# Six row tiles, DMA transposes and column tiles in a linear-attention and FFT-gate kernel on one core

## The chip, the core and the metric

The kernel runs on one core of one Trainium2 chip. The metric is the device time of one execution in microseconds (us). A core has a matrix engine (PE, with its weight loads shown as PEld), a vector engine (DVE), an activation engine (ACT), a general engine (POOL) and a queue engine (SP). They run their own instruction lists and wait for each other through semaphores. Matmul results go to PSUM, which DVE and ACT read; everything else works on SBUF. Transfers are issued from queues (here POOL's for loads, SP's and ACT's for stores) and carried by 16 DMA engines.

## What is computed

There are B = 8 batches, 8 heads, S = 576 positions and 64 columns a head, so 512 model columns. In the first half, attention without softmax:

```python
r = np.maximum(x, 0.0)
phi = np.concatenate([r * c, r * s], axis=-1)      # c, s: cosine and sine of the position
kv = np.einsum('bhsf,bhsd->bhfd', k_p, v)
z = np.sum(k_p, axis=2)
num = np.einsum('bhsf,bhfd->bhsd', q_p, kv)
den = np.einsum('bhsf,bhf->bhs', q_p, z)[..., None] + 1e-06
attn = num / den
```

In the second half, x is that result with its heads side by side, [8, 576, 512]:

```python
proj = x @ w_proj                                  # 512 x 1536
x1, x2, x3 = (three slices of 512 columns)
x2_conv = np.fft.irfft(np.fft.rfft(x2) * np.fft.rfft(filter), n=S)   # along the 576 positions
out = (x1 * x2_conv * x3) @ w_out
```

## The kernel before

The work is done batch by batch, and the batches are pipelined by hand: the order in which the program emits its pieces is, but for marked exceptions (`behind(...)` puts an instruction right after a marked one on its engine), the order of each engine. SBUF buffers and PSUM units (four, of two banks each) come from pools; a piece that asks for a buffer waits until its last reader is done.

Stages of a batch, with the names that the profile uses:

- **Loads.** POOL's queue loads q, k and v of a batch (`qraw`, `kraw`, `vraw`, L121) and casts them to f16. Position s = 6p + j lies in partition p, column group j.
- **phi** (L99, L97, on DVE): `kp` gets both halves by 12 instructions. `qp` gets a plain relu (one instruction of 3072 elements) and a second half scaled by the tangent (6 instructions).
- **kv** (L491): 48 matmuls for 8 heads; `va` is v with a column of ones beside it (copied by ACT, L128). ACT evicts to `kvs`.
- **qt** (L504): q is transposed by 48 matmuls against a permutation matrix `perm`, evicted in two overlapping halves by DVE (L511) and ACT (L515) into the single buffer `qpt`. The layout has five tiles of 128 columns, in which positions from the front and mirrored positions from the back stand side by side.
- **num** (L530): 40 matmuls, 5 tiles for each head. DVE adds epsilon, takes the reciprocal and multiplies into `att` (L536 to L540).
- **fx** (L556, L570, ACT L560, L574): matmuls against the small matrix `fm` transpose `att` and at the same time form 12 combinations of rows for a first radix-6 step of the FFT and 12 rows in plain order (front and back half). So one fold delivers both the operand of x2 and that of the gate.
- **x2** (L593): in three blocks of 96 rows and two components each, 24 matmuls of 512 columns. ACT scales into `x2f` (L598).
- **dft** (L607): 6 matmuls of 96x96 tables `tre` and `tim`; ACT copies to `xf`; DVE multiplies with the filter's spectrum `h3` (L612 to L617) into `yf`.
- **gate** (L630): x1 and x3 for four column groups, 64 matmuls of 288 columns. ACT copies x1 to f16 (`x1s`, L636); DVE multiplies it with x3, which it reads from PSUM (`g`, L638).
- **inv** (L656, L657): 32 matmuls with the inverse tables; ACT evicts to `eq` (L660); **y** (L672 to L677, DVE): even and odd sums (16 instructions of 144 elements for the four groups), the two halves, the product with `g`.
- **out** (L695): 20 matmuls against w_out on five row tiles, of which the last overlaps the one before; ACT evicts (L700), SP's queue stores in pieces that follow the row layout (L715).

The tables, among them those of the FFT, are computed on chip ahead of the loop. Batches 0 and 1 and the q part of batch 2 are emitted ahead of the loop, between the set-up pieces. The loop over b from 1 then emits x2 of b between num of b+1; dft of b; for each of the four column groups gate of b and fx of b+1; inv of b; out of b-1 between qt of b+2; kv of b+2; y of b. For the last batch `inv` is emitted ahead of the fourth gate, and its output tiles are evicted and stored tile by tile.

Of the kernel before, what the change touches and what calls it, by code (L numbers as in the profile page):

```python
# [17 lines left out]
def kernel(  # L18
# [15 lines left out]

    nc = tc.nc
# [6 lines left out]
    NT = 5  # L42
# [25 lines left out]
    tcol = consts.tile([128, NJ], FP32, tag="tcol", name="tcol")  # L68
    epsc = consts.tile([128, NT], FP32, tag="epsc", name="epsc")
    perm = consts.tile([NP, NP], FP16, tag="perm", name="perm")  # L70
# [5 lines left out]
    fm = consts.tile([128, 24, 10], FP16, tag="fm", name="fm")  # L76
    tre = consts.tile([NP, 3, NP], FP16, tag="tre", name="tre")
    tim = consts.tile([NP, 3, NP], FP16, tag="tim", name="tim")

# [9 lines left out]
    qpt_buf = [consts.tile([128, NH, NT, 2, 64], FP16, tag=f"qpt{i}", name=f"qpt{i}") for i in range(1)]  # L89
# [24 lines left out]
    raw_t = {}  # L114

    def load_qk(b, nm, hs=slice(0, NH)):
        src = {"q": q, "k": k, "v": v}[nm]
        if hs.start == 0:
            rw = work.tile([NP, NH, NJ * D], FP16, tag="raw", bufs=4, name=f"{nm}raw{b}")
            raw_t[(b, nm)] = rw  # L120
        nc.gpsimd.dma_start(  # L121
            out=raw_t[(b, nm)][:, hs], in_=src[b, hs].rearrange("h (p j) d -> p h (j d)", j=NJ)
        )

    def emit_va(b, xs=range(4)):
        for x in xs:
            hs = slice(2 * x, 2 * x + 2)
            nc.scalar.copy(  # L128
                out=va_buf[b % 2][:, hs, :, 0:D],
                in_=raw_t[(b, "v")][:, hs].rearrange("p h (j d) -> p h j d", j=NJ),  # L130
            )
# [28 lines left out]
    def emit_iotas(part):  # L160
# [13 lines left out]
        iota("sr_i", [NP, QS], lambda t: [(t, [[2, 3], [12, NP // 2]], 1, 0)])  # L174

    def emit_cols():
# [6 lines left out]
        nc.vector.memset(warm, 0.0)  # L183
        sj = cc["s6_i"]
# [3 lines left out]
        nc.vector.tensor_tensor(out=tcol, in0=tcol, in1=scol, op=AL.mult)  # L188

        u16 = small("u16p")  # L190
        rnd(u16, p, 1.0 / 16.0, -15.0 / 32.0)
        dest = small("dest")
        tsc(dest, p, 6.0, AL.mult)
        nc.vector.scalar_tensor_tensor(
            out=dest, in0=u16, scalar=-95.0, in1=dest, op0=AL.mult, op1=AL.add
        )
        tsc(perm, cc["nrow_i"], dest[0:NP], AL.is_equal)

    def emit_pads():
        for va in va_buf:  # L200
            nc.vector.memset(va[:, :, :, D : D + 2], 1.0 / A1)
        for t in qpt_buf:
            nc.vector.memset(t[:, :, :, 0, 60:64], 0.0)
            nc.vector.memset(t[:, :, :, 1, 0:4], 0.0)

    def emit_fm():

        p = cc["p"]
        loc = small("loc")
        side = small("side")  # L210
        nc.vector.tensor_copy(out=loc[0:64], in_=p[0:64])
        tsc(loc[64:128], p[64:128], -1.0, AL.mult, 127.0, AL.add)
        nc.vector.memset(side[0:64], 1.0)
        nc.vector.memset(side[64:128], -1.0)
        lo = small("lo")
        rnd(lo, loc, 1.0 / 6.0, -5.0 / 12.0)
        li = small("li")
        nc.vector.scalar_tensor_tensor(
            out=li, in0=lo, scalar=-6.0, in1=loc, op0=AL.mult, op1=AL.add
        )  # L220


        orb = small("orb", NT)
        for t in range(NT):
            tsc(orb[:, t : t + 1], lo, 10.0 * t, AL.add)
        oj = small("oj", NT)
        rnd(oj, orb, 1.0 / 16.0, -15.0 / 32.0)
        pos = small("pos", NT)

        tsc(pos, orb, 6.0, AL.mult)  # L230
        nc.vector.scalar_tensor_tensor(
            out=pos, in0=oj, scalar=-95.0, in1=pos, op0=AL.mult, op1=AL.add
        )
        nc.vector.scalar_tensor_tensor(
            out=pos, in0=li.to_broadcast([128, NT]), scalar=96.0, in1=pos, op0=AL.mult, op1=AL.add
        )
# [6 lines left out]
        orow_i = cc["orow_i"][:, 0:10]  # L243
        match = small("match", 10)
# [5 lines left out]
        for sl, (kk, c0) in enumerate([(0, 0.25), (3, 0.25), (1, 0.25), (1, 0.0), (2, 0.25), (2, 0.0)]):  # L250
# [4 lines left out]
        nc.scalar.activation(out=coef[:, 0:6], in_=ph, func=AF.Sin, scale=TWO_PI)  # L255
        tsc(coef[:, 3:6:2], coef[:, 3:6:2], 1.0 / R3, AL.mult)

        tsc(coef[:, 0:6], coef[:, 0:6], 2.0, AL.mult)
        tsc(coef[:, 0:6], coef[:, 0:6], RC, AL.add, -RC, AL.add)
        tsc(coef[:, 0:6], coef[:, 0:6], 0.5, AL.mult)  # L260
        tsc(coef[:, 6:12], coef[:, 0:6], side, AL.mult)
# [12 lines left out]
            in0=coef.unsqueeze(2).to_broadcast([128, 24, 10]),  # L274
            in1=match.unsqueeze(1).to_broadcast([128, 24, 10]),
# [23 lines left out]
    def emit_rows():  # L299
# [5 lines left out]
        par = cc["par"] = small("par")  # L305
        rnd(par, p, 0.5, -0.25)
        nc.vector.scalar_tensor_tensor(
            out=par, in0=par, scalar=-2.0, in1=p, op0=AL.mult, op1=AL.add
        )
# [10 lines left out]
    def emit_fwd_tables():  # L320
# [4 lines left out]
        u = small("u16")  # L325
        rnd(u, p, 1.0 / 16.0, -15.0 / 32.0)
        j = small("jr")
        nc.vector.scalar_tensor_tensor(
            out=j, in0=half, scalar=-3.0, in1=u, op0=AL.mult, op1=AL.add
        )  # L330
        w = small("w2s")

        tsc(w, p, 12.0, AL.mult, 1.0, AL.add)
        nc.vector.scalar_tensor_tensor(out=w, in0=u, scalar=-192.0, in1=w, op0=AL.mult, op1=AL.add)
        nc.vector.scalar_tensor_tensor(out=w, in0=j, scalar=2.0, in1=w, op0=AL.mult, op1=AL.add)
# [24 lines left out]
        for tb in (tre, tim):  # L360
            tsc(tb[:, 1:3], tb[:, 1:3], amp[0:NP], AL.mult)
            nc.vector.tensor_tensor(out=tb[:, 0], in0=tb[:, 0], in1=mask, op=AL.mult)

# [59 lines left out]
    def emit_h():  # L423
        hc, hs_, hb, alt = cc["hc"], cc["hs"], cc["hb"], cc["alt"]
        fa = filt16.rearrange("p x (j n) -> p x j n", j=3)
        for x, op in ((0, AL.add), (1, AL.subtract)):
# [5 lines left out]
        for bl in range(3):  # L432
# [15 lines left out]
            tsc(h3[:, bl, 1], u[0:NP, 1], sc, AL.mult)  # L448
            nc.vector.tensor_copy(out=h3[:, bl, 2], in_=h3[:, bl, 1])
        u = unit("h_nyq")  # L450
        for j in range(3):
            nc.tensor.matmul(
                u[0:1, 0], alt[:, j % 2 : j % 2 + 1], feo[:, 0, j], start=(j == 0), stop=(j == 2)
            )
        nc.scalar.activation(out=h3[0:1, 0, 2], in_=u[0:1, 0], func=AF.Copy, scale=1.0 / S)
# [4 lines left out]
    def emit_phi(b, nm, h0=0, nh=NH):  # L460
        rw = raw_t[(b, nm)]
        dst = kp_t if nm == "k" else qp_t
        if h0 == 0:
            dst[b] = work.tile([NP, NJ, NH, 2, D], FP16, tag=f"{nm}p", bufs=2 if nm == "q" else 1, name=f"{nm}p{b}")
        t = dst[b]
        if nm == "q":

            tsc(
                t[:, :, h0 : h0 + nh, 0],
                rw[:, h0 : h0 + nh].rearrange("p h (j d) -> p j h d", j=NJ), 0.0, AL.max,  # L470
            )
        for j in range(NJ):
            for cs, col in ((0, ccol), (1, scol)) if nm == "k" else ((1, tcol),):
                mark["phi", b, nm] = tsc(
                    t[:, j, h0 : h0 + nh, cs], rw[:, h0 : h0 + nh, ds(j * D, D)],
                    col[0:NP, j : j + 1], AL.mult, 0.0, AL.max,
                )
# [21 lines left out]
    def emit_qt(b, hp):  # L499
        qp, qpt = qp_t[b], qpt_buf[0]  # L500
        u = psum.tile([128, 2, 1024], FP16, tag="u", bufs=4, name=f"qt{b}_{hp}")
        for hh in range(2):
            for j in range(NJ):
                nc.tensor.transpose(  # L504
                    u[:, hh, ds(j * NP, NP)],
                    qp[:, j, 2 * hp + hh].rearrange("p a b -> p (a b)"),
                    perm,
                )
        hsl = slice(2 * hp, 2 * hp + 2)
        ev = nc.scalar.copy if b == 0 and hp < 2 else nc.vector.tensor_copy  # L510
        mark["qpt", b, hp] = ev(  # L511
# [368 lines left out]
```

## Time and profile before

| what | value |
|---|---|
| time, median of 3 | 272.12 us (272.1 to 272.9) |
| span of the profiled execution | 271.2 us |
| mean granted PE clock | 0.978 |
| busy share PE / DVE / ACT | 90% / 84% / 73% |
| length of a steady batch period | 28.5 us |
| DMA, mean over the span | 98 GB/s |

A busy share is an average over the whole span. Matmuls are pipelined, so a group's mean duration (for instance 286 ns for the gate's) is the way through the array, while the spacing of their starts is what a queue of them costs. Sums over a stretch of the chain of waits, divided by their number of instructions, give that spacing. Idle time in a group's row is that of its engine just ahead of the group, with what ended most of it.

### The profile page before, as it was taken

What the parts mean: (1) busy time and instruction counts of PE and PEld (TensorE: products, weight loads), DVE (VectorE), ACT (ScalarE), POOL (GpSimd) and SP (SyncE); (2) the same over time, 40 slices, a digit from 0 to 9 for tenths busy, and PEclk for the clock granted to TensorE, in tenths of its full rate; (3) what the DMA queues carried; (4) which work ended last, traced back from release to release, by engine and by line L of the source; (5) the groups of instructions that cost most, each with busy time, mean ns of one, the idle gap of its engine ahead of it and who ended that gap; (6) DMA issues with size and microseconds to landing.
All of it is one profiled execution on the core that took longest, in us unless ns stands there. A gap on an engine that the chain in (4) does not pass through costs nothing.

```text
span 271.2 us, 6320 instructions
## 1 busy us (share of the span) xinstructions
PE 243.0 (90%) x2457; PEld 175.2 (65%) x2457; DVE 226.9 (84%) x805; ACT 196.8 (73%) x274; POOL 27.3 (10%) x47
## 2 busy tenths in 40 slices
PE   0287998878989999999999999999999999999991
PEld 0164767547858776786678676867687768756830
DVE  7689997998899898979897989978997479646951
ACT  2279679798497778877897789786977667857630
POOL 8551111020020101110111011000000000000000
PEclk9999999995799999999999999999999999999998
DMA  5999998919019296636860868114000600060235
GB/s 79 168 206 205 206 205 122 166 14 169 3 14 161 33 230 90 89 40 152 150 101 3 174 128 124 16 51 125 0 2 9 169 2 0 2 174 13 69 117 155
DMA packets 26991, 26.70 MB, mean 98 GB/s; under 512 B 1680, under 2 KB 22160, under 8 KB 26960
## 3 DMA queue, kind: packets, MB, share of 16 engines
q0 software_dynamic: 21200, 16.84, 42.7%
q1 hardware_dynamic: 5120, 8.39, 10.7%
q10 hardware_dynamic: 640, 1.05, 1.3%
q8 instruction: 19, 0.31, 0.5%
q14 instruction: 12, 0.10, 0.1%
HBM read 33.69 MB, written 9.44 MB: 159 GB/s over the span
## 4 chain that ended last, share of the span: by engine, by line
PE 50%; ACT 22%; DVE 21%; DMA 4%; issue 1%; POOL 0%; SPq 0%; POOLq 0%; ACTq 0%
PE x L630 20%; PE x L593 9%; ACT x2f L598 7%; ACT va L128 7%; PE kv L491 5%; PE out L695 4%; PE fx L556 4%; DVE eo L672 4%; ACT fx L560 3%; DMA vraw<-in_v_dram 2%; DVE kp L99 2%; PE qt L504 2%; PE dft L607 2%; PE inv L657 2%; DVE qpt L511 2%; PE inv L656 2%
## 5 line engine op out<-in xcount | busy, mean ns | idle before, releaser
L630 PE MATMUL x<-fx,wp 128*128 128x288 f16 x512 | 67.5, 286 | 1.1 <-ACT fx L560 1.0
L630 PEld LDWEIGHTS <-wp 128*128 128x128 f16 x512 | 50.0, 98 | 13.3 <-issue 0.3
L593 PE MATMUL x<-wp,fx 128*96 128x512 f16 x192 | 45.2, 382 | 0.5 <-ACT x2f L598 0.5
L560 ACT CAST fx<-fx 128x960 f16<-128x960 f32 x32 | 30.6, 961 | 13.7 <-PE fx L556 13.7
L695 PE MATMUL out<-wo,y 128*128 128x512 f16 x160 | 37.6, 379 | 0.7 <-DVE y L677 0.7
L598 ACT ACTIVATE x2f<-x 96x1024 f16<-96x1024 f32 x24 | 24.5, 1020 | 14.6 <-PE x L593 14.6
L593 PEld LDWEIGHTS <-fx 128*96 128x96 f16 x192 | 22.4, 124 | 15.1 <-issue 0.8
L672 DVE TENSOR_TENSOR eo<-eq 128x144 f16<-128x144 f16 x128 | 23.7, 228 | 10.1 <-ACT eq L660 9.9
L128 ACT COPY va<-vraw 96x768 f16<-96x768 f16 x32 | 25.3, 827 | 9.3 <-DMA vraw<-in_v_dram 9.3
L638 DVE TENSOR_TENSOR g<-x,x1s 128x288 f16<-128x288 f32 x64 | 27.0, 448 | 1.3 <-PE x L630 1.1
L491 PE MATMUL kv<-va,kp 96*128 96x65 f16 x384 | 16.4, 202 | 11.7 <-ACT va L128 8.8
L540 DVE TENSOR_TENSOR att<-num,rcp 128x640 f16<-128x640 f32 x32 | 26.1, 820 | 0.3
L515 ACT COPY qpt<-qt 128x600 f16<-128x600 f16 x32 | 20.4, 671 | 7.5 <-DVE qpt L511 7.5
L695 PEld LDWEIGHTS <-y 128*128 128x128 f16 x160 | 14.9, 97 | 16.0 <-DVE y L677 1.2
L609 ACT CAST xf<-dft 96x1024 f16<-96x1024 f32 x24 | 23.5, 1010 | 2.2 <-PE dft L607 1.2
L491 PEld LDWEIGHTS <-kp 96*128 96x128 f16 x384 | 15.3, 104 | 13.3 <-DVE kp L99 8.1
L504 PEld LDWEIGHTS <-qp 96*128 96x128 f16 x384 | 20.2, 102 | 5.1 <-issue 1.1
L636 ACT CAST x1s<-x 128x576 f16<-128x576 f32 x32 | 20.5, 639 | 4.2 <-PE x L630 3.1
L612 DVE TENSOR_TENSOR m<-xf,h 96x1024 f16<-96x1024 f16 x24 | 16.3, 678 | 7.8 <-ACT xf L609 7.7
L504 PE MATMUL qt<-perm,qp 96*128 96x96 f16 x384 | 21.7, 213 | 0.5 <-ACT fx L560 0.3
L700 ACT ACTIVATE os<-out 128x1024 f32<-128x1024 f32 (+1 forms) x21 | 18.3, 883 | 5.2 <-PE out L695 5.1
L556 PE MATMUL fx<-fm,att 128*128 128x240 f16 x128 | 18.8, 270 | 2.2 <-DVE att L540 1.1
(185 smaller groups left out, 419.4 us busy)
## 6 DMA issues: line engine op xcount, KB each, us to landing
out_dram<-os SPq DMA_DIRECT2D x22, 192.0 KB, 2.5
qraw<-in_q_dram POOLq DMA_DIRECT2D x7, 576.0 KB, 6.6
kraw<-in_k_dram POOLq DMA_DIRECT2D x7, 576.0 KB, 6.3
vraw<-in_v_dram POOLq DMA_DIRECT2D x7, 576.0 KB, 6.5
out_dram<-os SPq DMA_DIRECT2D x20, 128.0 KB, 2.4
wp<-in_moe_w_proj_dram POOLq DMA_DIRECT2D x3, 512.0 KB, 12.3
out_dram<-os SPq DMA_DIRECT2D x22, 64.0 KB, 2.1
kraw<-in_k_dram POOLq DMA_DIRECT2D x2, 288.0 KB, 6.4
```

The costliest lines, as they stand in the source:

```text
L128: nc.scalar.copy(out=va_buf[b % 2][:, hs, :, 0:D], in_=raw_t[(b, "v")][:, hs].rearrange("p h (j d) -> p h j d", j=NJ),)
L491: nc.tensor.matmul(u[:, h // 4, ds((h % 4) * 65, 65)], kp[:, j, h].rearrange("p a b -> p (a b)"), va[:, h, j, 0:65], start=(j == 0), stop= ...
L504: nc.tensor.transpose(u[:, hh, ds(j * NP, NP)], qp[:, j, 2 * hp + hh].rearrange("p a b -> p (a b)"), perm,)
L540: mark["att", b, hp] = nc.vector.tensor_tensor(out=att[:, :, ds(hp * 128, 128)].rearrange("p t (h d) -> p h t d", h=2), in0=nv[:, :, :, 0: ...
L556: nc.tensor.matmul(u[:, t // 2, 0:480].rearrange("p (g o) -> p g o", o=20)[:, :, ds((t % 2) * 10, 10)], att[:, t, ds(c * 128, 128)], fm, s ...
L560: nc.scalar.copy(out=fx[:, c, :, 0:40].rearrange("p g (u o) -> p u g o", u=2), in_=u[:, :, 0:480].rearrange("p u (g o) -> p u g o", o=20),)
L593: nc.tensor.matmul(u[0:NP, comp], fx[:, c, ds(comp * 6 + 2 * bl, 2)].rearrange("p a b -> p (a b)"), wp16[:, c, ds(DM, DM)], start=(c == 0) ...
L598: mark["x2f", b, bl] = nc.scalar.mul(out=x2f[:, bl], in_=u[0:NP], mul=X2SC)
L630: nc.tensor.matmul(u[:, hf, 0:HS], wp16[:, i, ds(w * DM + c * 128, 128)], fx[:, i, ds(12 + 6 * hf, 6)].rearrange("p a b -> p (a b)"), star ...
L638: mark["g", b, c] = nc.vector.tensor_tensor(out=(g[:, c, 0:HS] if hf == 0 else g[:, c, HS:S][:, ::-1]).rearrange("p (j i o) -> p j i o", j ...
L672: nc.vector.tensor_tensor(out=eoh[:, a, :, ds(48 * x, 48)], in0=eqj[:, a, 0], in1=eqj[:, a, 1], op=op)
L695: nc.tensor.matmul(u[:, x], y[:, c, ds(OT[t], 128)], wo16[:, c], start=(c == 0), stop=(c == NC - 1),)
```

## The change

It has five parts, and a new order of the pieces around them.

1. **Row layout.** Six tiles of 96 positions take the place of five of 128 with mirrored halves (`NT = 6`). qt uses an identity for j < 3 and a swap of neighbouring partitions for j >= 3; the position order of the output becomes such that a store's segment is 48 rows.
2. **DMA transposes.** From batch 2, q is loaded in three pieces (two of them with neighbouring partitions swapped), `qp` has a new order, and four DMA transposes on SP's queue write `qpt`. The gate's operand is no longer made by the fold: one DMA transpose of `att` writes `xt` (`XT_DMA` batches 2 to 7). The fold makes only the 12 rows for x2. Batches 0 and 1 keep matmul transposes and make both by two folds.
3. **x2 in row tiles of 128.** The 576 rows of x2 are four tiles of 128 and one of 64 (the last one as two halves of the contraction, written to the two halves of PSUM). Since a tile no longer coincides with a DFT block, zero-padded copies of the tables (`tpad`) are made ahead of the loop by small DMAs, and a batch's DFT takes 9 matmuls.
4. **Column tiles.** In `out` the last 64 rows are computed as two halves of 256 columns in the two halves of PSUM.
5. **Balance and tail.** x3 is copied to f16 by ACT (`x3s`) ahead of the product; `eo` takes half as many instructions; two of four va copies of a batch go to DVE from batch 3; the filter spectrum's eviction goes to ACT; for the last batch inv comes ahead of the third gate, each output tile has its own buffer, evictions are split between DVE and ACT, and stores alternate between the SP and ACT queues.

```diff
-    NT = 5
+    NT = 6
+    tpad = [consts.tile([128, NP], FP16, tag=f"tpad{i}", name=f"tpad{i}") for i in range(7)]
+    XT_DMA = (2, 3, 4, 5, 6, 7)
+    DMA_QT = 2
...
+        if nm == "q" and b >= DMA_QT:
+            nc.gpsimd.dma_start(out=rw[:, hs, 0 : 3 * D], in_=view[:, :, 0 : 3 * D])
+            for x in range(2):
+                nc.gpsimd.dma_start(
+                    out=rw[x::2, hs, 3 * D : 6 * D], in_=view[1 - x :: 2, :, 3 * D : 6 * D]
+                )
...
     def emit_qt(b, hp):
+        if b >= DMA_QT:
+            nc.sync.dma_start_transpose(
+                out=qpt[:, hsl].rearrange("p h (j n) -> p (h j) n", j=NJ),
+                in_=qp[:, hsl].rearrange("p h j a b -> p (h j a b)"),
+            )
+            return
...
     def emit_num(b, hp, wm=0):
             for t in range(NT):
+                m = NP if hh and t >= 4 else 128
+                c0 = h * S + 2 * NP * (t // 2) + t % 2
                 nc.tensor.matmul(
-                    u[:, hh, ds(t * 65, 65)], qpt[:, h, t].rearrange("p a b -> p (a b)"),
+                    u[0:m, hh, ds(t * 65, 65)], qpt[:, c0 : c0 + 2 * m - 1 : 2],
...
+    def emit_xt(b):
+        xt_t[b] = work.tile([128, NT, NC, NP], FP16, tag="xt", bufs=2, name=f"xt{b}")
+        nc.sync.dma_start_transpose(
+            out=xt_t[b].rearrange("p t c n -> p (t c) n"),
+            in_=att_t[b].rearrange("p t n -> p (t n)"),
         )
...
     def emit_x2(b, bls=range(3)):
+            if bl < 2:
+                for x in range(2):
+                    for c in range(NC):
+                        mm(u[:, x], 2 * bl + x, 128, c, range(NC))
+            else:
+                for c in range(2):
+                    for x in range(2):
+                        mm(u[ds(64 * x, 64), 0], 4, 64, c + 2 * x, range(2 * x, 2 * x + 2))
...
+    DFT = (
+        ((tre[:, 0], 0),), ((tpad[0], 0), (tpad[1], 1)), ((tpad[2], 1), (tpad[3], 2)),
+        ((tpad[4], 2),), ((tre[:, 2], 3),), ((tpad[5], 3), (tpad[6], 4)),
+    )
...
     def emit_gate(b, c):
-                        fx[:, i, ds(12 + 6 * hf, 6)].rearrange("p a b -> p (a b)"),
+                        xt[:, i, ds(6 * hf, 6)].rearrange("p a b -> p (a b)")
+                        if b not in XT_DMA else xt[:, :, i, ds(48 * hf, 48)],
...
+            x3s = work.tile([128, 2, HS], FP16, tag="x3s", bufs=2, name=f"x3s{b}_{c}")
+            nc.scalar.copy(out=x3s, in_=us[1][:, :, 0:HS])
...
     def emit_y(b, c):
-            for a in range(2):
-                nc.vector.tensor_tensor(
-                    out=eoh[:, a, :, ds(48 * x, 48)], in0=eqj[:, a, 0], in1=eqj[:, a, 1], op=op
-                )
+            nc.vector.tensor_tensor(
+                out=eoh[:, :, :, x], in0=eqt[:, :, 0], in1=eqt[:, :, 1], op=op
+            )
...
     def emit_out(b, grps=OG):
+                if t == 4 and not last:
+                    for c in range(NC):
+                        for hf in range(2):
+                            nc.tensor.matmul(
+                                u[ds(64 * hf, 64), x, 0 : DM // 2], y[:, c, 512:576],
+                                wo16[:, c, ds(hf * (DM // 2), DM // 2)],
+                                start=(c == 0), stop=(c == NC - 1),
+                            )
...
+                    if last:
+                        q_ = (nc.sync, nc.scalar)[store[0] % 2]
...
     (in the loop over b)
         if nx:
             emit_num(n, 2)
+        if b < B:
+            emit_dft(b, (0,))
+        if nx:
             emit_num(n, 3)
+            if n in XT_DMA:
+                emit_xt(n)
...
+            with behind(*(("yf", 0, 2) if b == 1 else ("g", b - 1, NC - 1))):
                 emit_phi(n + 1, "q")
+            for x in range(4):
+                emit_qt(n + 1, x)
...
+                with behind("eo", b, 3):
+                    emit_va(n + 1, (0, 1))
+                with behind("g", b, 0):
+                    emit_va(n + 1, (2, 3), nc.vector.tensor_copy)
```

## The prediction

> **What bounds the kernel now.** I read the page first (busy shares, then the shares of the chain of waits), then the windows of busy time with one window per batch, then the chain in order of time, then the groups of instructions by form, then the queues.
>
> ```profile
> span 271.2 us, 6320 instructions
> PE 243.0 (90%) x2457; PEld 175.2 (65%) x2457; DVE 226.9 (84%) x805; ACT 196.8 (73%) x274; POOL 27.3 (10%) x47
> PE 50%; ACT 22%; DVE 21%; DMA 4%; issue 1%; POOL 0%; SPq 0%; POOLq 0%; ACTq 0%
> ```
>
> ```profile
> 100.80:129.30 28.50, 27.89 (x303) 20.67 (x302) 25.76 (x85) 23.04 (x31) 2.48 (x3) 1.00 0.59 99
> 129.30:157.76 28.46, 27.85 (x303) 20.66 (x302) 25.64 (x84) 23.03 (x31) 2.32 (x3) 1.00 0.63 113
> ```
>
> The columns after the length are PE, weight loads, DVE, ACT and POOL busy, the granted clock, the DMA share. The middle of the kernel is a steady period of 28.5 us per batch in which PE is busy 27.9 us, DVE 25.7, ACT 23.0. A busy PE need not be a full one, so I price its work by the spacing of its matmuls, which the chain of waits shows:
>
> ```profile
> 78.75 0.88 PE dft L607 x4
> ...
> 94.41 0.51 PE qt L504 x12
> ...
> 99.08 1.68 PE kv L491 x48
> 100.76 1.76 PE x L593 x8
> ...
> 108.95 1.96 PE x L630 x16
> 110.92 0.41 PE fx L556 x4
> ```
>
> So a dft matmul takes 0.22 us, qt 0.0425, kv 0.035, x2 0.2175 (1.74/8), gate 0.1225, fold (fx) 0.1025; out is 0.2175 (1.73 for 8), inv 0.0625 (starts 0.06 apart in the timeline), num 0.031 (20 in 0.78, less the last one's 0.19). A batch is gate 64: 7.84; x2 24: 5.22; out 20: 4.35; qt 48: 2.04; inv 32: 2.00; kv 48: 1.68; fold 16: 1.64, its remainder 4: 0.31; dft 6: 1.32; num 40: 1.24. Sum 27.6 of 28.5 us: PE is full, only 0.9 us per period is waiting. DVE comes next, ACT has 5 us of room.
>
> ```profile
> L560 ACT CAST fx<-fx 128x960 f16<-128x960 f32 x32 | 30.6, 961 | 13.7 <-PE fx L556 13.7
> L638 DVE TENSOR_TENSOR g<-x,x1s 128x288 f16<-128x288 f32 x64 | 27.0, 448 | 1.3 <-PE x L630 1.1 <-ACT x1s L636 0.2
> L540 DVE TENSOR_TENSOR att<-num,rcp 128x640 f16<-128x640 f32 x32 | 26.1, 820 | 0.3
> L515 ACT COPY qpt<-qt 128x600 f16<-128x600 f16 x32 | 20.4, 671 | 7.5 <-DVE qpt L511 7.5
> L675 DVE TENSOR_TENSOR y<-eo 128x288 f16<-128x288 f16 x32 | 9.7, 304 | 0.2
> ```
>
> ```profile
> q0 software_dynamic: 21200, 16.84, 42.7%
> q1 hardware_dynamic: 5120, 8.39, 10.7%
> ```
>
> The tail, at the end of the chain, is a wait for store buffers: the last y is ready at 261.46, the span ends at 271.2, and stores stand on the chain.
>
> ```profile
> 263.67 0.60 ACT os L702
> ...
> 265.02 1.89 DMA out_dram<-os
> 266.91 0.69 DVE os L97
> ```
>
> **What the Trainium skill says.** (1) "DMA: Bandwidth & Descriptors", section "Latency and other measured facts", gives a DMA transpose 261 GB/s with a non-contiguous middle dimension and 350 to 400 contiguous; "VectorE: DVE Perf Modes", section "The three transpose paths", gives 1309 ns for one 128x128 block. No transpose by DMA is in this trace, so nothing here confirms either. (2) "DMA: Bandwidth & Descriptors", section "Issuing engines are not separate DMA queues": all issues share the same 16 engines, so transposes add to loads and stores; the queue lines above show what is there already. (3) "TensorE: Matmul & The Clock Gate", section "Measured speedup vs the span model": three column tiles ran 2.38 times as fast; "TensorEngine Tiling (Array Packing)", section "Key Properties", adds that changing the tiling mode drains the array. The kernel before has no such matmul. (4) "VectorE: DVE Perf Modes", section "Why PSUM operands drop a tier": an operand in PSUM loses a fast mode. The trace agrees: 288 columns cost 448 ns from PSUM f32 (L638), 304 ns from f16 in SBUF (L675).
>
> **The change part by part**, for a steady batch.
>
> PE. The q transposes go to DMA from batch 2: -2.04. The fold makes only the 12 x2 rows, 24 matmuls of 96 columns in place of 16 of 240 and 4 of 192; the nearest row is qt (same 96 rows and 96 columns, 0.0425), so 1.02 for 1.95: -0.93. x2 in row tiles of 128: 16 full matmuls, 3.48, and 4 of 64 columns that write the two halves of PSUM. If the halves run side by side these are 0.43, one after the other 0.87; I take 0.65 for the drains. 4.13 for 5.22: -1.09. DFT with padded tables: 9 matmuls for 6: +0.66. num: 48 for 40: +0.25. out: the last 64 rows as 8 matmuls of 256 columns in two column halves, 0.43 to 0.87, 0.65 taken for 0.87: -0.22. Gate, kv and inv are unchanged; the gate reads its moving operand in six runs of 48, which I cost at nothing since the old one was also made of runs of 48 through a different view. Sum -3.4 (ends -2.9 and -3.8): 24.2 us of PE work.
>
> DVE. Gone: four copies of qpt, 4 x 0.465 = 1.86. g from f16: 8 x (0.448 - 0.304) = -1.15. eo in 8 instructions of 288 in place of 16 of 144: 8 x 0.304 - 16 x 0.228 = -1.22. att over six tiles: 4 x 0.82 x 0.2 = +0.66. Half of the va copies come from ACT: +0.6 (a quarter of the 3072-element relu's 947 ns, with a fixed part, is 0.3 each). relu in two: 2 x 0.546 - 0.947 = +0.15. Sum -2.8: 22.9.
>
> ACT. qpt -2.68; fold 4 x 0.65 for 4 x 0.961 + 0.81: -2.05; va -1.65; x3s copies 4 x 0.64 = +2.56; x2f's last tile -0.42; os -0.2. Sum -4.4: 18.6. (0.65 is L636's 639 ns for the same 576 elements.) The new x3s work lies beside the gate matmuls: with the x2 tail, two dft blocks and the folds these four steps take PE 11 us, while ACT needs 2 x 0.93 for xf, 12 x 0.57 for x1s, x3s and folds and 0.55 for x2f, 9.3.
>
> Queues. SP gets, in this order per batch: the transpose of att (xt), four of q (qt), then 17 stores. xt waits for att(n), qt for num(n) to have read the single qpt buffer. Queued behind them are the stores of the batch before; they wait for nothing else, and the os buffers are asked for again only a period later. xt is wanted a period later, qt about 15 us later by num(n+1). Bytes: 96 x 6144 x 2 = 1.18 MB and 0.59 MB, 1.77 MB: 6.8 us at 261 GB/s, 4.4 at 400. The loads' packet time is 42.7% of 271.2 us for 16.84 MB, so 12.2 us for a batch's 1.77 MB; the stores take (10.7 + 1.3)% over 8 batches, 4.1. With 6.8 that is 23 us of 25, so DMA is nearly full but does not bind if the price holds. The three-part load of q has runs half as long; at the worst it costs its 4.1 us again, and then DMA would be at 27 us (counted under B).
>
> So the period is PE's 24.2 plus the same 0.9 of waiting, 25.1. Five periods (those that hold a q transpose of batches 3 to 7) gain 3.4 each: 17.0. The period of batch 6, with no q transpose before either: 0.93 + 1.09 + 0.22 - 0.66 - 0.25 = 1.3. Batch 7: 0.65. Ahead of the loop: batch 2's qt 2.04, x2(0) 1.09, less 0.66 and two times 0.35 for num and two fold halves: 1.8; set-up adds about 20 small DVE instructions at 0.15, 3 us, part of them ahead of the first fold: I take -1.5 for these, and nothing for the stretch of reduced clock between 61 and 75 us. Tail: after the last y 14 matmuls (3.0), half an eviction (0.4), issue and a 2.4 us store, about 6.5 for 9.7, and two gates now cover the y chain: 4. Sum 17.0 + 1.3 + 0.65 + 0.3 + 4 = 23.2. DVE, with 22.9 of 25.1 a little tighter than now (91% for 90%), gives back perhaps 0.2 per period, 1.2. 272.1 - 22.0 = 250.
>
> **Rivals.** A (0.60): as above, 250. B (0.25): DVE or ACT in order becomes the bound, because kv, num, att and dft now share a shorter period; periods of 26.8 in place of 25.1 for six batches give 260. For it: DVE's 91%, and six-tile att lying ahead of dft's products. Against it: the work of both falls. C (0.10): the transposes bind. At one block of 128x128 in 1.309 us, 72 blocks one after another would be 94 us; the break-even for a 25 us period is 71 GB/s. If they run at 50 GB/s, 35 us per batch, five periods of 35.4 give 250 + 5 x 10.3 = 301, slower than before. For it: nothing in the trace prices them. Against it: the skill's 261. D (0.05): the column halves run side by side without drains, the clock stays full, 244.
>
> **How the numbers follow.** The time is A's, 250. Range 242 to 266: D, A and B with an error of 6 us on B; C is left out. Faster by over 0.3%: A, B, D less a little, 0.88; slower is C, 0.10; same 0.02.
>
> **What would show it.** Windows per batch near 25 us with PE busy about 24.3, DVE 23, ACT 18.6; no PE group for qt beyond 96 matmuls; g near 300 ns; the waits for qpt on PE near zero, and SP's transposes landing within 5 us each. It is wrong if PE waits for a DMA into qpt or xt (then C), if DVE's windows are full while PE waits for att or yf (then B), or if the pairs of 64-column matmuls take longer than full ones.

## The result and the profile after

| | before | after |
|---|---|---|
| time, median (lowest to highest) | 272.3 us (272.1 to 272.9), 4 runs | 244.86 us (244.16 to 246.69), 4 runs |
| ratio, 95% interval | | 0.8999, 0.8943 to 0.9056 |
| profiled span, granted clock | 271.2 us, 0.978 | 242.4 us, 0.991 |

The forecast was 250.0, range 242 to 266. Ratios here and below leave out executions more than 1.5% longer than the shortest of their kernel, while medians and ranges count all. The first view is the page of the kernel after: span, busy shares, the rows of the clock and of the DMA share, and the shares of the chain of waits.

```profile
span 242.4 us, 6225 instructions
PE 218.4 (90%) x2333; PEld 151.2 (62%) x2333; DVE 212.3 (88%) x747; ACT 178.8 (74%) x275; POOL 35.3 (15%) x61
PEclk9998899999999999999999999999999999999999
DMA  5999999799999959999999999999495524063315
PE 76%; ACT 11%; DVE 6%; DMA 4%; issue 1%; POOL 1%; ACTq 0%; POOLq 0%
```

PE's busy share is 90% as before, and that says nothing about what happened. The shares of the chain do: PE holds 76% of it where it held 50%, DVE 6% where it held 21%, ACT 11% where it held 22%. The windows, one per period (from one start of kv to the next), show it plainly. The columns are as in the prediction.

```profile
115.60:139.81 24.21, 24.21 (x271) 17.09 (x272) 23.56 (x75) 19.16 (x29) 3.54 (x6) 1.00 1.22 193
139.81:164.02 24.21, 24.21 (x271) 17.09 (x272) 23.56 (x75) 19.16 (x29) 2.44 (x4) 1.00 1.18 198
```

PE is busy 24.21 us of 24.21: no waiting at all is left, where 0.6 of 28.5 us was left before. DVE is busy 23.56, ACT 19.16. The last but one column is the DMA share, 1.18 to 1.22 where it was about 0.6; since it passes 1, it must count packets that are under way side by side. The chain in time through the first of these periods (start, length, engine, operation, line, number):

```profile
115.60 1.63 PE kv L543 x48
117.23 1.73 PE x L648 x8
118.96 0.80 PE num L584 x24
119.75 1.73 PE x L648 x8
121.48 0.40 PE num L584 x12
121.88 0.66 PE dft L680 x3
122.54 0.40 PE num L584 x12
122.94 0.55 PE x L648 x4
123.50 0.78 PE dft L680 x3
124.27 1.96 PE x L713 x16
126.23 0.65 PE dft L680 x3
126.89 0.26 PE fx L611 x6
...
135.80 3.46 PE out L785 x16
139.25 0.56 PE out L803 x8
139.81 1.63 PE kv L543 x48
```

Each start is the end of the piece before it: a queue of matmuls without a gap. The four gate pieces are 1.96 each as before, so the operand from `xt` costs no more than the old one. No `qt` is left, four pieces of fold take 0.26 each, the 64-row tail of x2 takes 0.55, that of out 0.56. The groups that answer to those shown of before (busy time in the whole run, mean ns, idle time ahead):

```profile
L626 ACT CAST fx<-fx 128x576 f16<-128x576 f32 x32 | 20.5, 640 | 5.5 <-PE fx L611 5.5
L738 DVE TENSOR_TENSOR g<-x3s,x1s 128x288 f16<-128x288 f16 x64 | 17.5, 298 | 4.3 <-ACT x3s L723 4.2
L594 DVE TENSOR_TENSOR att<-num,rcp 96x768 f16<-96x768 f32 x32 | 30.4, 948 | 0.4
```

The fold's eviction fell from 961 to 640 ns, `g` from 448 to 298, and `att` rose from 820 to 948 with its sixth tile. The queues (packets, MB, share of the packets' time in 16 engines' span):

```profile
q0 software_dynamic: 26000, 16.85, 51.2%
q1 hardware_dynamic: 49792, 19.56, 43.0%
```

SP's queue q1 now has 49792 packets for 5120, and 43.0% for 10.7%: most of these are the transposes (without any, in experiment 3, it has 7360 and 11.7%). At the end of the run, the timeline of the kernel after (start, length, engine, line, operation; in brackets the idle time ahead and who ended it):

```profile
234.92 1.83 ACTq L842 DMA_DIRECT2D out_dram<-os  x4
236.79 0.38 ACT L823 ACTIVATE os<-out 128x256 f32<-128x256 f32 x1 [3.85 <-DVE os L105]
237.15 0.85 ACTq L842 DMA_DIRECT2D out_dram<-os  x2
238.04 0.38 ACT L823 ACTIVATE os<-out 128x256 f32<-128x256 f32 x1 [0.87 <-DVE os L105]
238.46 0.86 ACTq L842 DMA_DIRECT2D out_dram<-os  x2
```

The last matmuls end at 237.2 and the span at 242.4. ACT's two evictions stand in one queue with its own store issues, so the last starts at 238.04, after two issues that take 0.85 us.

Where the 28.8 us between the two profiled spans lie, read from the starts of kv and of the last x2:

| piece | before | after | gain | forecast |
|---|---|---|---|---|
| to kv of batch 2 | 68.59 | 67.82 | 0.8 | 0.3 |
| first period (to kv of batch 3) | 30.49 | 23.50 | 7.0 | 3.4 |
| four periods, to kv of batch 7 | 114.0 | 96.8 | 17.2 | 13.6 |
| period of batch 6, to the last x2 | 26.1 | 24.3 | 1.8 | 1.3 |
| batch 7 and the tail | 32.0 | 30.0 | 2.1 | 4.65 |
| given back to DVE | | | none | -1.2 |

The profiled execution of the kernel after is the shortest of its four and that of before the longest of its four; by the medians the gain is 27.4 us.

The first two rows are best read together, 7.8 us for a forecast of 3.7. In the kernel after, 16 of the 20 matmuls of x2 of batch 1 (3.63 us, from 62.37) stand ahead of kv of batch 2; in the kernel before all of them stand behind it. The windows of the first period, before and after:

```profile
68.59:99.08 30.49, 29.46 (x304) 21.90 (x303) 28.05 (x99) 22.27 (x30) 2.42 (x3) 0.95 0.48 79
67.82:91.32 23.50, 21.21 (x256) 15.52 (x254) 23.46 (x80) 19.25 (x30) 2.78 (x4) 1.00 1.14 152
```

After the change DVE is busy for all of it (23.46 of 23.50 us) and PE only for 21.21. PE's 2.3 us of waiting lie in its first 6.6 us, where DVE is full. So DVE sets the start of this one period, unlike the later ones.

### The profile page after: what moved, and what is told of

Its sections match the earlier page's. It is cut to its first block, busy times and chain, and to the rows that moved or that the text cites. A ratio compares the mean times of both kernels' runs of the same rounds, so it can differ in the third digit from the quotient of the medians.

```text
span 242.4 us, 6225 instructions
## 1 busy us (share of the span) xinstructions
PE 218.4 (90%) x2333; PEld 151.2 (62%) x2333; DVE 212.3 (88%) x747; ACT 178.8 (74%) x275; POOL 35.3 (15%) x61
## 3 DMA queue, kind: packets, MB, share of 16 engines
q1 hardware_dynamic: 49792, 19.56, 43.0%
## 4 chain that ended last, share of the span: by engine, by line
PE 76%; ACT 11%; DVE 6%; DMA 4%; issue 1%; POOL 1%; ACTq 0%; POOLq 0%
PE x L713 26%; PE x L648 12%; PE out L785 11%; PE dft L680 6%; PE kv L543 4%; PE num L584 4%; PE fx L611 3%; PE inv L750 3%; PE inv L749 3%; ACT va L145 3%; DMA vraw<-in_v_dram 3%; DVE att L594 2%; PE out L803 2%; PE qt L563 2%; PE num L535 1%
## 5 line engine op out<-in xcount | busy, mean ns | idle before, releaser
L713 PE MATMUL x<-xt,wp 128*128 128x288 f16 x512 | 67.3, 286 | 0.0
L648 PE MATMUL x<-wp,fx 128*128 128x512 f16 (+1 forms) x160 | 35.4, 381 | 2.2 <-DVE qpt L569 1.6
L666 ACT ACTIVATE x2f<-x 128x1024 f16<-128x1024 f32 (+1 forms) x24 | 21.2, 885 | 17.1 <-PE x L648 17.1
L594 DVE TENSOR_TENSOR att<-num,rcp 96x768 f16<-96x768 f32 x32 | 30.4, 948 | 0.4
L785 PE MATMUL out<-wo,y 128*128 128x512 f16 (+1 forms) x132 | 30.3, 379 | 0.0
L723 ACT CAST x3s<-x 128x576 f16<-128x576 f32 x32 | 20.4, 638 | 8.5 <-PE x L713 8.0
L626 ACT CAST fx<-fx 128x576 f16<-128x576 f32 x32 | 20.5, 640 | 5.5 <-PE fx L611 5.5
L738 DVE TENSOR_TENSOR g<-x3s,x1s 128x288 f16<-128x288 f16 x64 | 17.5, 298 | 4.3 <-ACT x3s L723 4.2
L764 DVE TENSOR_TENSOR eo<-eq 128x288 f16<-128x288 f16 x64 | 17.5, 299 | 2.5 <-ACT eq L753 2.5
L584 PE MATMUL num<-kvs,qpt 128*128 128x65 f16 (+1 forms) x384 | 17.5, 200 | 1.9 <-DVE rcp L593 1.1
L611 PEld LDWEIGHTS <-att 96*128 96x128 f16 x240 | 13.6, 98 | 7.8 <-DVE att L594 3.5
## 6 DMA issues: line engine op xcount, KB each, us to landing
kraw<-in_k_dram POOLq DMA_DIRECT2D x7, 576.0 KB, 10.3
```

What stands on the lines that cost most here:

```text
L584: nc.tensor.matmul(u[0:m, hh, ds(t * 65, 65)], qpt[:, c0 : c0 + 2 * m - 1 : 2], kvs[:, h // 4, ds((h % 4) * 65, 65)], start=True, stop=True,)
L594: mark["att", b, hp] = nc.vector.tensor_tensor(out=att[:, :, ds(hp * 128, 128)].rearrange("p t (h d) -> p h t d", h=2), in0=nv[:, :, :, 0: ...
L611: nc.tensor.matmul(dst.rearrange("p (g e o) -> p g e o", e=2, o=8)[:, :, e], att[:, 2 * j + e, ds(c * 128, 128)], fm[0:NP, gs], start=True ...
L626: mark["fx", b] = nc.scalar.copy(out=dst[:, c].rearrange("p g (j o) -> p j g o", j=3), in_=uf[:, 0:768].rearrange("p (j g o) -> p j g o", ...
L648: nc.tensor.matmul(dst, fx[:, c].rearrange("p g o -> p (g o)")[:, ds(128 * ch, n)], wp16[:, c, ds(DM, DM)], start=(c == cs[0]), stop=(c == ...
L666: mark["x2f", b, bl] = nc.scalar.mul(out=x2f[:, 2 * bl : 2 * bl + n], in_=u[:, 0:n], mul=X2SC)
```

## The experiments

The theory under test is that the time is PE's own work, 24.2 us a period, and each part of the change is worth what it takes from PE. Against it: that DVE (or ACT) in its order sets the period and the PE work follows, and that the DMA transposes set it. Experiments 1 to 9 are edits of the kernel after; 10 is one of the kernel before. All ratios are to the kernel before on the same chip. There it takes 270.4 to 271.7 us (medians) for the 272.3 of the result, so a difference in us to the kernel after can be off by one or two; lengths of periods and ratios are safer. No run adds a part of the change alone to the kernel before: all but experiment 10 take something out of the kernel after, or add to it, in its order of pieces.

### 1 and 3: q back on PE, without and with the gate operand

```diff
-    DMA_QT = 2
+    DMA_QT = 8
```

> The changed kernel, but q of every batch is transposed by matmuls (attention output still by DMA). Theory 1 (PE is the bound, its period is the sum of its matmul spacings): 48 matmuls of 0.0425 us come back, period 24.21 + 2.04 = 26.25 us, with batch 2 ahead of the loop 6 x 2.04, 257 us. Theory 2 (the gain came from DVE and ACT evictions that went away, PE only follows): DVE gets 4 x 0.45 us back, 23.56 + 1.8 = 25.4, so a period of 25.4 and 251 us. Theory 3 (DMA holds the period): less DMA traffic, so no slower than 245.

Measured: 270.37 us (268.62 to 272.77, 20 runs), ratio 0.999, 0.9962 to 1.0018. The 48 q matmuls, 2.04 us a period, cost not 2 but 4.1 us a period: of the four steady periods two are 28.3 us long, one is 29.9 (at a granted clock of 0.94) and one 27.7. With that, the whole gain is gone, although the rest of the change is there (only the loads of q are in one piece again). The waits of PE in the steady stretch (engine, line, what it waited for: us, times, longest), and then the chain in time through part of two periods, the first of them 28.3 us long:

```profile
PE out L785 <- DVE qpt L569: 6.5, 4, 1.9
```

```profile
122.80 0.38 DVE qpt L569
123.22 3.61 PE out L785 x16
126.83 0.56 PE out L803 x8
127.39 1.63 PE kv L543 x48
129.02 1.73 PE x L648 x8
130.75 0.41 PE num L584 x12
131.38 0.23 DVE rcp L593
131.66 0.94 DVE att L594
...
151.06 0.38 DVE qpt L569
```

Between the last two lines the chain stays on DVE (att, the products for yf, g, kp, y), and only then returns to PE. So the loop goes over both engines: some 8 us of PE from that copy to num, and 20 us of DVE from there to the next copy. PE is busy 26.4 us of a period of 28.3 and waits for the rest. In this variant all 48 q matmuls stand together ahead of out, where the kernel before had them between the three groups of out. How much of the 4.1 us is that order was not separated.

```diff
-    XT_DMA = (2, 3, 4, 5, 6, 7)
-    DMA_QT = 2
+    XT_DMA = ()
+    DMA_QT = 8
```

> No DMA transposes at all: q and the gate's operand by matmul in every batch. Theory 1: period 24.21 + 2.04 + 1.04 = 27.3 us, 263 us. Theory 2: DVE 25.4, ACT 24.3: period 25.4, 251 us. If waits return beside the work, period 28 and 267 us.

Measured: 271.08 (269.81 to 272.4, 12 runs), ratio 1.0009, 0.9979 to 1.0039; periods 28.2 to 28.4. The gate operand back on PE adds a microsecond of matmuls per batch and changes nothing in the period; PE's waits for `qpt` in the steady stretch fall from 6.5 to 3.4 us instead. In a period set by the loop over DVE, this PE work is free.

### 2: the gate operand alone back on PE

```diff
-    XT_DMA = (2, 3, 4, 5, 6, 7)
+    XT_DMA = ()
```

> The changed kernel, but the gate's operand of every batch comes from a second fold by matmul, as in batches 0 and 1 (q still by DMA). Theory 1: 24 matmuls of 0.0433 us come back, period 24.21 + 1.04 = 25.25 us, six batches, 251 us. Theory 2: DVE's work is the same, ACT gets 2.6 us and stays at 21.8, so the period stays 24.2 and the time 245. Theory 3: 245 or a little less.

Measured: 251.39 (250.72 to 253.91, 4 runs), ratio 0.9297, 0.9219 to 0.9375; periods 25.29. Four pieces of 12 fold matmuls take 0.51 for 0.26 each, 1.0 us, and the period grows by 1.08. Here, where PE is full, the same microsecond counts in full, in each of six batches. Beside experiment 3 this is the clearest pair: one edit, worth 6.5 us by the medians (3.0% by the ratios) with PE full, and nothing that can be measured with DVE's loop in charge.

### 4: the tail of x2 without the two halves

```diff
-                for c in range(2):
-                    for x in range(2):
-                        mm(u[ds(64 * x, 64), 0], 4, 64, c + 2 * x, range(2 * x, 2 * x + 2))
+                for c in range(NC):
+                    mm(u[0:64, 0], 4, 64, c, range(NC))
```

The eviction and the last DFT table are cut to 64 rows with it.

> The last 64 rows of x2 as four matmuls in one column half with the whole contraction, in place of two pairs in the two halves. Theory 1: 0.87 us in place of the 0.55 measured, period 24.53, eight batches, 2.5 us more: 247.4. If the pairs do not run side by side but one after the other, no change: 245. Theory 2: no change: 245.

Measured: 248.83 (248.36 to 250.37, 4 runs), ratio 0.9196, 0.9144 to 0.9247; periods 24.87, 0.66 more. The chain of this variant:

```profile
124.51 0.98 PE x L648 x4
125.49 0.78 PE dft L679 x3
126.27 1.96 PE x L712 x16
128.23 0.78 PE dft L679 x3
129.00 0.36 PE fx L611 x6
```

The four matmuls take 0.98 for 0.55: the two halves do run side by side. The starts of the matmuls say the same: in the kernel after, the two of a pair start 0.003 us apart, here the four start 0.216 to 0.240 apart. A direct reading gives 0.43 of the 0.66. The other 0.23 lies in the next pieces: the last dft 0.78 for 0.65, the fold behind it 0.36 for 0.26. There the last dft matmul of this variant contracts over 64 rows between others over 128 and 96. The step from the matmul ahead of it is 0.309 us and the step from it to the fold 0.346, where these steps are 0.22 in the kernel after. So the 0.2 us lies at this one matmul; that it comes of the 64 rows was not tested apart.

### 5 and 6: work put onto PE, and onto DVE

Three matmuls of 512 columns ahead of each kv from batch 3; their result is overwritten.

```diff
+        for x in range(3 if b >= 3 else 0):
+            nc.tensor.matmul(u[:, 0], wp16[:, 0, 0:128], wp16[:, 0, 0:512], start=True, stop=True)
```

> The changed kernel with three more matmuls of 512 columns ahead of kv of batches 3 to 7 (their result is overwritten). Theory 1 (PE bound without a gap): each period grows by 3 x 0.2175 = 0.65 us, 5 periods, 3.3 us: 248. If another engine or the DMA set the period, less than half of that.

Measured: 249.32 (248.09 to 250.75, 4 runs), ratio 0.9181, 0.9118 to 0.9245; periods 24.86, 0.65 more, which is three times the 0.217 us that a 512-column matmul takes in a queue. PE work goes into the period one to one. The median is 4.5 us up, more than five times 0.65. In the profile 3.3 us of the excess lie ahead of the first added matmul: kv of batch 2 starts at 71.09 for 67.82, and between 43 and 71 us the granted clock is 0.88. That part is not what the added matmuls cost in the periods.

On DVE, the two halves of y are computed twice for three of four column groups, 1.3 us a batch.

```diff
+        if 1 <= b <= 6 and c < 3:
+            nc.vector.tensor_tensor(out=y[:, c, 0:HS], in0=eo[:, 0], in1=eo[:, 1], op=AL.add)
+            nc.vector.tensor_tensor(out=y[:, c, HS:S][:, ::-1], in0=eo[:, 0], in1=eo[:, 1], op=AL.subtract)
```

> The two halves of y are computed twice for three of four column groups of batches 1 to 6: 6 DVE instructions of 0.22 us spacing, 1.3 us per batch. Theory 1: DVE has 0.65 us free in a period of 24.21, so the period becomes DVE's: 24.86, about 6 x 0.65 = 3.5 us in all at most, 247 to 248.5; PE shows waits again. Theory 2 (DVE set the period already): 1.3 us each, 252. If DVE has more room than its busy share shows: 245.

Measured: 247.22 (246.63 to 247.46, 4 runs), ratio 0.9105, 0.9046 to 0.9164; periods 24.78, 0.57 more for 1.3. What PE waits for in the steady stretch of this variant, in the first line:

```profile
PE num L584 <- DVE rcp L590: 0.8, 3, 0.4
```

DVE had 0.65 us free (24.21 less 23.56); 1.3 less 0.65 is 0.65, and the period grew by nearly that. The first of these periods grew by 1.2, nearly the whole; there DVE was busy 24.11 us of 24.28 in the kernel after. DVE is the second bound and stands very close.

### 7: work put onto ACT

```diff
-                    emit_va(n + 1, (0, 1))
+                    for _ in range(3):
+                        emit_va(n + 1, (0, 1))
```

The two va copies that ACT still has are made three times, 3.0 us more a batch.

> ACT's two va copies of batches 4 to 7 are made three times, 4 more copies of 0.75 us spacing, 3.0 us per batch. Theory 1: ACT has 5 us free, so the period stays within 0.3 us of 24.21: 245 to 246. If the order of ACT's queue matters (evictions of out stand behind the copies, and kv waits for them): up to 3 us each, 257.

Measured: 251.27 (248.69 to 251.86, 4 runs), ratio 0.9233, 0.9162 to 0.9304; later periods 25.47, 1.26 more. ACT has 5 us free in a period and takes 3, so by the sum nothing should have changed. What PE waits for in two of the later periods:

```profile
PE kv L543 <- ACT va L145: 2.1, 4, 0.9
```

The copies stand in ACT's queue shortly ahead of the kv that needs them; what delays them delays kv. Idle time in a window is not room at every place in the queue.

### 8: a transpose more

A second transpose of att into a tile that nobody reads, right behind the first (the last batch has three output buffers in place of five, for the space).

```diff
+        nc.sync.dma_start_transpose(
+            out=xd.rearrange("p t c n -> p (t c) n"),
+            in_=att_t[b].rearrange("p t n -> p (t n)"),
+        )
```

> The transpose of the attention output is made twice (the second time into a tile that nobody reads), 0.59 MB more per batch; the last batch has three output buffers in place of five to make room, which can cost the tail 1 us. Theory 1: DMA and the SP queue have room (SP issues about 17.6 of 24.2 us, 21 with this), the steady period stays 24.21: 245 to 246. Theory 3 (DMA is at its limit, its row is at nine tenths all through the middle): the period grows by up to the transfer's 3.5 us, 4 to 6 of them, 259 to 266.

Measured: 258.25 (253.47 to 262.91, 4 runs), ratio 0.9397, 0.9288 to 0.9505. The shortest is 8.6 us over the median of the kernel after. In the profile (of the longest run) two periods are 34.6 and 33.0 us and the others 24.2, and PE waits there for the q transposes:

```profile
PE num L585 <- DMA qpt<-qp: 13.5, 5, 4.2
```

In the kernel after, the fourth q transpose of the period shown above, for the last two heads, is issued at 134.8. The view of this one transpose has its time to landing:

```profile
L555 SPq DMA_TRANSPOSE qpt<-qp x1: 1859/1859/1859, 134.8 to 134.8; - x1
DMA to landing us min/median/max: 8.8/8.8/8.8
```

The first three land after 3.6 to 3.9 us, this one at 143.7, and the fourth piece of num, which reads it, starts at 146.6. So 2.9 us are to spare; in the periods before and behind it is 3.9 and 2.4. The issue of one more transpose of att takes 3.1 to 4.0 us of SP's queue ahead of q's, about all of that. So the transposes did not bind, but stood next to it. Both the queue and the engines have a part: in the first long period of the variant the fourth q transpose is issued at 117.6 for 110.4 in the kernel after, and then takes 12.0 us to land for 8.0.

### 9: x3 read from PSUM again

```diff
-    X3_ACT = (0, 1, 2, 3)
+    X3_ACT = ()
```

> From batch 2 DVE reads x3 from PSUM again and ACT makes no f16 copy. Theory 1: DVE gets 8 x 0.15 = 1.2 us, 24.76 against PE's 24.21, so the period becomes DVE's: 0.55 us more, five or six periods, 248; ACT's 2.3 us less bring nothing. If DVE has hidden room: 245. If x1s alone on ACT shortens the way to g: below 245.

Measured: 247.61 (246.01 to 250.06, 4 runs), ratio 0.9137, 0.9076 to 0.9197; periods 24.68, 0.47 more, with DVE busy 24.50 us of them. What this puts back on DVE (1.2 us by durations, 0.9 by its busy time) is again paid for only where DVE's 0.65 us of room ends, as in experiment 6. So ACT's copy of x3 was worth 0.5 us a period, because PE is faster now; by the same sum it would be worth nothing beside a PE of 28 us, which was not run.

### 10: the stretch of reduced clock in the kernel before

```diff
-        emit_num(1, hp)
+        emit_num(1, hp, 2)
```

Two extra matmuls ahead of each of the four pieces of num of batch 1, whose result is overwritten, keep PE busier there.

> The kernel before, with two idle matmuls of 512 columns ahead of each num of batch 1, where PE waits for DVE at about 50 to 56 us. If the reduced clock between 61 and 75 us comes of those waits: the clock stays full, 1 to 2.5 us faster than before, 270 to 271. If not: the same or up to 1.7 us slower, 272 to 274.

Measured: 270.46 (268.88 to 272.61, 20 runs) beside 270.52, ratio 0.9993, 0.9969 to 1.0017: no gain. The reduced slices of the clock row rose from 5 and 7 tenths to 8 and 8, and the first period shrank from 30.49 to 29.81 in the profile. So extra matmuls ahead of the loop take no time away. That the dip itself costs nothing is not shown: of the 27 executions of the kernel before on this chip, the seven with a mean granted clock of 0.978 or 0.979 took 271.9 to 273.7 us, and the twenty from 0.988 up took 269.3 to 270.8. The kernel before was profiled in an execution at 0.978.

### 11 and 12: the tail, and va on POOL

```diff
-                    nv = DM if t == 4 else DM // 2
+                    nv = DM
```

DVE alone evicts the last output tiles.

> The changed kernel, with the evictions of the last batch's tiles all on DVE, none behind the store issues on ACT's queue. If ACT's issues (which wait for an earlier store's end) hold up the last evictions: the stretch from the last matmul to the end goes from 5.2 to about 4.6 us, 0.6 us faster, 244.3. If not: 0.3 us slower, since the last tile's eviction on one engine takes 0.27 us longer.

Measured: 245.17 (242.65 to 254.28, 7 runs), ratio 0.9011, 0.8955 to 0.9066, beside 0.8999 for the kernel after: no difference. The tail of the profile agrees: from the last matmul to the end of the span it is about 5.0 us for 5.2. With ACT's queue out of the way, the eviction on DVE is 0.69 us long, and the store behind it is most of what remains. The profiled execution is the longest of the seven and tells nothing about the edit, but it shows what a late transpose does. The chain there:

```profile
117.06 13.71 DMA qpt<-qp
...
130.81 0.90 PE num L584 x12
```

One q transpose took 13.71 us to land, all of PE's spare time and more: PE waits 6.9 us for it in that period, runs part of it at a lower clock, and the period is 34.5 us long. Two of the four q transposes of that batch also held SP's queue for 4.4 and 3.6 us at their issue, for 1.3 to 1.9 as a rule. Why is open.

With the same tail, half of the va copies of batches 1 and 2 went to POOL.

```diff
-        emit_va(1)
+        emit_va(1, (0, 1))
+        emit_va(1, (2, 3), nc.gpsimd.tensor_copy)
```

> As the tail variant, and half of the va copies of batches 1 and 2 go from ACT to the idle POOL engine. Between 43 and 62 us ACT is busy without a gap (19.37 of 19.37 us). If ACT sets the pace there: 4 copies of 0.73 us less on it, up to 2.9 us, 241.5 to 243. If POOL's copies are much slower than ACT's (over 2 us each) or hold up the loads behind them in POOL's queue: slower than the tail variant.

Measured: 249.75 (246.12 to 258.59, 6 runs), ratio 0.9122, 0.9062 to 0.9181: by the ratios about 1% slower than experiment 11, with intervals that just meet. ACT is busy without a gap from 43 to 62 us in the kernel after, just ahead of the loop, but this move does not help. In its profile (of one of the longer executions, 252.13 us) kv of batch 2 starts at 72.6 for 67.8 in the kernel after. From 43 to 62 us ACT is busy only 14.2 us and PE 18.96 of 19.00, at a granted clock of 0.85 for 1.00. So ACT was relieved, and the time shows as PE work at a lower clock; why the clock is lower there is open. No variant is measurably faster than the kernel after.

## Why the forecast was right, and where it was off

**PE's work: right.** 24.2 forecast, 24.21 measured. By parts, forecast and measured: x2 4.13 and 4.01, out 4.13 and 4.02, dft 1.98 and 2.09, num 1.49 and 1.60, fold 1.02 and 1.04, q none. The only doubtful terms were the two tails of 64 columns, taken at 0.65 between 0.43 and 0.87; they are 0.55 and 0.56, and experiment 4 shows that one of them would be 0.98 in a row. So the halves run side by side. The starts show what comes on top of 0.43: the step from num into the tail of x2 is 0.142 us, and 0.047 into full matmuls; the step out of it to dft is 0.309 and the next one 0.253, for the usual 0.22. Together that is 0.2 us, and with it the tail costs the 0.65 that was forecast; but a part is counted in the pieces beside it, so x2 came out below its forecast and dft and num above. It agrees with the statement of the Trainium skill, "TensorEngine Tiling (Array Packing)", section "Key Properties", that a change of the tiling mode drains the array; that it is the drain, no run shows. The saving is 3.7 and not 3.4 because the work of before was summed to 27.6 and the windows had 27.9; a sum from spacings should have been checked against that row.

**The waiting: the largest term that was mis-sized.** The forecast carried the old 0.9 us of waiting over to the new period; it was 0.6 before and is 0 now. The list of waits of PE in four periods of before (99.08 to 213.08):

```profile
PE kv L491 <- ACT qpt L515: 1.3, 4, 0.3
PE dft L607 <- ACT x2f L598: 1.1, 4, 0.3
```

After, PE waits for neither. The first went with its cause. For the second there is a likely reason: in the kernel before ACT makes four copies of va between its three of `x2f`, in the kernel after they stand elsewhere, two of them on DVE. No run tests it. With 0.3 of PE work this is 0.9 of a period that was not forecast, 3.6 us in four periods. And the 1.2 us set aside for DVE were not needed.

**The q transposes: right in the sum, worth more in the new order.** The forecast priced them by their matmuls, 2.04. Experiment 1 shows 4.1 us a period in the new order, since with them comes a round trip between PE and DVE. In the order of the kernel before, that trip cost little: PE waited 0.3 us a period behind the copies of `qpt`. So the forecast's price held for the step from before to after, and the other 2 us belong to the new order with q on PE. How they split between the trip and the place of the q matmuls stays open.

**DVE: 22.9 forecast, 23.56 measured.** The mis-sized term is `eo`, counted by durations: 16 x 0.228 for 8 x 0.304, 1.22. DVE instructions overlap; three short ones take 0.51 us in the timeline of before, so one starts each 0.14, and the new ones start each 0.22 in the chain of experiment 1 (three in 0.65). 16 x 0.14 less 8 x 0.22 is 0.5, and the missing 0.7 is there. ACT is 19.2 for 18.6. Rival B did not come in the steady periods, but it was close: DVE stands 0.65 us below PE there, experiments 6 and 9 cross that line, and the start of the first period is DVE's.

**DMA: not binding, as said, but for half the right reason.** The forecast took 261 GB/s for the transposes from the Trainium skill, "DMA: Bandwidth & Descriptors", section "Latency and other measured facts", 6.8 us a batch. Measured by q1's packet time between variants: the transposes of att take (0.192 x 267.8 - 0.117 x 269.9) / 6 = 3.3 us each, 179 GB/s (experiment 1 less 3), those of q (0.307 x 250.1 - 0.117 x 269.9) / 6 = 7.5 us a batch, 157 GB/s (experiment 2 less 3). That is 10.8 us. In the kernel after, where both run, q1's packet time less that of experiment 3 is 12.1 us a batch. With the loads the DMA share passes 1 and still does not bind; what counts is when the last q transpose lands, and that is 2.4 to 3.9 us ahead of its reader in the three steady periods that have loads beside them. The forecast's sign, that the transposes land within 5 us each, did not come: those of att take 5.7 us (median), the last of q 8.0 to 9.3. Rival C falls for the kernel after, and experiment 8 shows how near it was.

**The ends: both wrong.** Batch 7 and the tail were to give 4.65 and gave 2.1: after the last y (233.7) it took 8.7 us, not 6.5, because the last 16 matmuls, ACT's eviction behind its own store issues and the store follow each other. Experiment 11 shows that taking ACT out of it gains nothing: DVE's eviction is longer. The first period gained 7.0, not 3.4. Some 2 us of it is how far the first period of before stood over its steady one, with a granted clock of 0.88 in its first 12 us; experiment 10 could take 0.7 of that away in a profile, and no time. The new first period is 0.7 shorter than the later ones because 3.6 us of its matmuls stand ahead of it; it is not shorter still because DVE is full at its start. The forecast had neither. That this error and the tail's go opposite ways, 3.6 us too little and 2.6 too much, is luck.

## What to carry to other kernels

A step is worth its instructions and the round trip that goes with it, and the second depends on the order around it: the same q matmuls came with 0.3 us of waits in the kernel before and cost 2 us more than themselves in the new order. So ask which engine evicts the result, what stands ahead of that eviction in that engine's order, and who waits for it. Once a change makes one engine full without a gap, a small edit is worth very nearly what it takes from that engine, up to where the next engine is full, and the same edit is worth nothing where a loop over two engines sets the period (experiments 2 and 3). Before relying on a transfer that is "hidden", compare the time at which it lands with the time at which its reader asks, for the last of the transfers and not for the median, and not the busy share of the DMA engines.

## What the runs showed of the hardware that was not expected

- A DMA transpose holds the issuing queue: 2.9 to 3.7 us for the one of att (0.59 MB), 1.3 to 1.9 us for each of four of q (0.29 MB) in the steady periods. They land after 5.7 and 4.3 us (medians), but the last of the four of q after 8.0 to 9.3 in the three steady periods with loads beside them, and after 3.7 in the next one, where the DMA share is 0.75.
- The transposes move in packets of about 250 bytes (3.54 MB in 14016 packets, experiment 1 less 3). Loads of v beside them land later: 8.8 us (median), 6.9 in experiment 3, which has no transposes. The loads of k land after 10.3 us, but in experiment 3 after 9.7, for 6.3 in the kernel before; so with k it is mostly not the transposes.
- Four matmuls of 64 columns by 512, in pairs on the two halves of PSUM, take 0.55 us; in a row 0.98, where four full ones take 0.87. In a row they start as far apart as full ones (0.216 to 0.240); the surplus lies in the steps into and out of the group (0.142 for 0.047, 0.309 for 0.22), and the pairs have the same steps.
